# RetNet attention and a SwiGLU block in one kernel: the RMS norm's power taken of three columns with tokens on the partitions, and brought back as rows

## The chip, the cores and the metric

The kernel runs on one core of a Trainium2 chip. The metric is the device time of one execution in microseconds (us), the median of several runs. A core has five engines with queues of their own: TensorE (PE, matrix products; PEld is its weight load), VectorE (DVE), ScalarE (ACT), GpSimd (POOL) and SyncE (SP, which here only issues transfers). Each engine works through its own queue in order; they wait for one another by semaphores. SBUF is the on-chip memory of 128 partitions, PSUM the banks that TensorE writes its products to.

## What is computed

A retention block for 8 batches, 8 heads, 576 tokens and 64 columns a head, then an RMS norm and a SwiGLU block over the 4608 tokens that come of it (512 columns, 1536 inner columns). The reference, cut to what matters:

```python
scores = scale * np.matmul(q, k.transpose(0, 1, 3, 2))        # per batch and head
Dmat = np.where(rel >= 0, gamma[:, None, None] ** rel, 0.0)   # causal decay
x = np.matmul(scores * Dmat, v)                               # -> (4608 tokens, 512)

rms = np.sqrt(np.mean(x * x, axis=-1, keepdims=True) + 1e-06)
xn = x / rms * rms_g
g = xn @ w_gate
silu = g * (1.0 / (1.0 + np.exp(-g)))
out = silu * (xn @ w_val) @ w_out
```

The change touches only the lines with `rms` and `xn`: one power (mean of squares + 1e-6) to -0.5 for each of the 4608 tokens, and the multiplication of x by it.

## The kernel before

**Tiles.** All values are fp32. The tokens are worked through in 12 units (u = 0 to 11) of U = 384 tokens. Within a unit x lies transposed: model columns on the 128 partitions, in four tiles c of 128 columns each, tokens along the row (`x[:, c]` is 128x384). A sum over a token's 512 columns is therefore a sum over partitions.

**Attention** is cut into 32 jobs (batch, pair of heads), worked in `slot(j)`: scores and states of job j, values and carried part of job j-1, then the transposes of job j+1 (`prepare`) and the loads of job j+2 (`load`). The last step of a job writes its columns of x for the units that its tokens belong to.

**The SwiGLU block of a unit.** `up(u, m, g)` runs six times (i = 0 to 5: three groups g, gate and value). Each is seven block products of a Strassen-like scheme, named x, y, z, x, w, z, w after their PSUM banks, each of four matrix products of 128x192; the trace shows eight instructions for one block product, since an fp32 product is two instructions. Sums and differences of the products are DVE's, SiLU is ACT's. Then `down(u, s)` runs three times (s = 0, 1, 2), each 12 products of 128x512 (24 instructions) into one bank, a copy by ACT and a transfer out.

**The norm of the next unit** is spread over the end of a unit by `behind(u, i)`: `norm_0(u+1)` is written after the sixth `up`, `norm_1(u+1)` after `down(u, 0)`, `norm_2(u+1)` after `down(u, 1)`; `down(u, 2)` comes after that, and then `up(u+1)`. For u = 0 the three follow one another with nothing between.

- `norm_0` squares the four tiles on ACT and adds them on DVE (three additions) to one tile of 128x384.
- `norm_1` multiplies that by a matrix of 1/512 on TensorE (L298), so that each partition of the bank `ms` holds the means of all 384 tokens; DVE adds 1e-6 (L300, tile `r`), and POOL raises the 128x384 elements to -0.5 (L301).
- `norm_2` multiplies x by the gain and by `r` (L307, four DVE instructions), and forms the four differences that the block products need (L316, tile `sums` and x in place).

**What sets the order.** The program is written out in the order of its instructions: each engine gets its own in the order in which the loops above write them, and nothing reorders them. `SLOTS` says after which i of a unit a slot of the attention stands: units with u % 3 = 0 have four (after i = 0, 2, 4, 5), u % 3 = 1 has one (after i = 6, which is `down(u, 0)`, and ahead of `norm_1`), u % 3 = 2 has three (1, 3, 5).

**Weights.** The weights come in 36 chunks and are decoded on DVE and ACT from 64-bit words (`exponent`, `mantissa`, `join`), with some sums on POOL (L502). This ends within unit 0 and is written between the pieces of its `up`.

**PSUM.** Five banks of one pool are taken in turn by `bank(...)`; three more hold the scores.

Of the kernel before, what the change touches and what calls it, by code (L numbers as in the profile page):

```python
# [8 lines left out]

F32 = mybir.dt.float32  # L10
U32 = mybir.dt.uint32
AF = mybir.ActivationFunctionType
ALU = mybir.AluOpType
P = 128
# [6 lines left out]
def _decay_tables(H, D):  # L21

    pairs = _gamma(H).reshape(H // 2, 2).T
    rows = np.repeat(pairs, D, axis=0)
    pos = np.arange(P)
    twice = np.concatenate([pos, pos])
    t = rows[:, :, None] ** twice / np.sqrt(D), pairs.T[None] ** -pos[:, None, None], rows ** -(pos % D)[:, None], rows**P
    return [np.ascontiguousarray(x).astype(np.float32) for x in t]  # L30


def _causal_tables():

    t = np.triu(np.ones((P, P), np.float32))
    return [t, np.ascontiguousarray(np.tile(t[: P // 2, : P // 2], (2, 1)))]
# [3 lines left out]
def kernel(  # L40
# [11 lines left out]
    nc = tc.nc  # L52
    B, H, S, D = q.shape
    NTOK, DM = out.shape
# [7 lines left out]
    SQ = 32  # L62
    U = 384
    HU = U // 2
    NU = NTOK // U
    NH = NF // 2
    NG = NH // 2
    EPS = 1e-6
    assert (D, DM, NHP * P) == (64, H * D, DM) and S % SQ == 0 and NTOK % U == 0
    assert NC == NFULL + 1 and TAIL == 64 and AC * P == U and NHP == 4 and NH % 2 == 0  # L70
    assert (2 * S) % U == 0 and B % 2 == 0 and S == 3 * HU

    const = ctx.enter_context(tc.tile_pool(name="const", bufs=1))
# [4 lines left out]
    tmp = ctx.enter_context(tc.tile_pool(name="tmp", bufs=6))  # L78
# [4 lines left out]
    def bank(name):  # L83
        return banks.tile([P, 512], F32, tag="b", name=name)

    def temp(name):
        return tmp.tile([P, U], F32, tag="t", name=name)

    def cell(name, value):
        t = const.tile([P, 1], F32, name=name)  # L90
        nc.vector.memset(t, value)
        return t

    ones = const.tile([P, P], F32, name="ones")
    mhalf = cell("mhalf", -0.5)
    least = cell("least", -896.0)
    most = cell("most", 255.0)
# [8 lines left out]
    rms_g = const.tile([P, NHP], F32, name="rms_g")  # L106
    w_out = const.tile([P, NF, DM], F32, name="w_out")
    o_all = const.tile([P, 2, DM], F32, name="o_all")
# [15 lines left out]
    x_of, t_of, h_of = {}, {}, {}  # L124
# [3 lines left out]
    def load(j):  # L128
        b, hp = jobs[j]
        for nm, src in (("q", q), ("k", k)):  # L130

            t = raw.tile([P, S // SQ, SQ], F32, tag=nm + "raw", name=f"{nm}raw_{j}")
            for e in range(2):
                rows = src[b, 2 * hp + e].rearrange("(t b) (i a) -> i b t a", b=SQ, a=SQ)
                for i in range(D // SQ):
                    r = e * D + i * SQ
                    nc.sync.dma_start(out=t[r : r + SQ], in_=rows[i])
            st[j][nm + "raw"] = t


        for nm, src, bufs in (("k", k, 2), ("v", v, 3)):
            t = raw.tile([P, NFULL, 2, D], F32, tag=nm, name=f"{nm}_{j}", bufs=bufs)
            for e in range(2):
                nc.sync.dma_start(
                    out=t[:, :, e],
                    in_=src[b, 2 * hp + e, : NFULL * P].rearrange("(c p) d -> p c d", p=P),
                )
            st[j][nm] = t
        t = st[j]["vt"] = raw.tile([P, D], F32, tag="vt", name=f"vt_{j}", bufs=3)
        for e in range(2):  # L150
            nc.sync.dma_start(
                out=t[e * TAIL : e * TAIL + TAIL], in_=v[b, 2 * hp + e, NFULL * P :]
            )

    def prepare(j):

        d = st[j]
        hp = jobs[j][1]
        for nm in ("q", "k"):
            t = att.tile([P, S], F32, tag=nm + "T", name=f"{nm}T_{j}")  # L160
            nc.vector.transpose(out=t, in_=d.pop(nm + "raw").rearrange("p t a -> p (t a)"))  # L161
            d[nm + "T"] = t
        for e in range(2):
            t = d["v"][:, :, e]
            nc.scalar.activation(out=t, in_=t, func=AF.Copy, scale=gv[:, hp, e : e + 1])
        nc.scalar.activation(out=d["vt"], in_=d["vt"], func=AF.Copy, scale=gt[:, hp : hp + 1])
# [76 lines left out]
    def carried(j):  # L243
# [4 lines left out]
        for c in range(1, NC):  # L248
# [4 lines left out]
            )  # L253
        for q0 in range(0, S, HU):
            blk, o = divmod(q0, AC * P)
            u, c0 = divmod(b * S + q0, U)
            if u not in x_of:
                x_of[u] = xp.tile([P, NHP, U], F32, tag="x", name=f"x_{u}")
            nc.vector.tensor_tensor(
                out=x_of[u][:, hp, c0 : c0 + HU], in0=av[blk][:, o : o + HU],  # L260
                in1=gq[:, hp, q0 % P : q0 % P + HU], op=ALU.mult,
            )
        st[j] = {}

    def slot(j):

        if j > len(jobs):
            return
        if j < len(jobs):
            scores(j)  # L270
            states(j)
        if j > 0:
            values(j - 1)
        if j < len(jobs):
            weigh(j)
        if j > 0:
            carried(j - 1)
        if j + 1 < len(jobs):
            prepare(j + 1)
        if j + 2 < len(jobs):  # L280
            load(j + 2)
# [13 lines left out]
    def norm_1(u):  # L295

        ms = bank(f"ms_{u}")
        nc.tensor.matmul(ms[:, :U], lhsT=ones, rhs=t_of[u], start=True, stop=True)  # L298
        r = t_of[u] = temp(f"r_{u}")
        nc.vector.tensor_scalar(out=r, in0=ms[:, :U], scalar1=EPS, scalar2=None, op0=ALU.add)  # L300
        nc.gpsimd.tensor_tensor(out=r, in0=r, in1=mhalf.to_broadcast([P, U]), op=ALU.pow)  # L301

    def norm_2(u):

        x = x_of[u]
        for c in range(NHP):
            nc.vector.scalar_tensor_tensor(  # L307
                out=x[:, c], in0=x[:, c], scalar=rms_g[:, c : c + 1], in1=t_of[u],
                op0=ALU.mult, op1=ALU.mult,
            )  # L310
        b11, b12 = x[:, :2, :HU], x[:, :2, HU:]
        b21, b22 = x[:, 2:, :HU], x[:, 2:, HU:]
        t = ffn.tile([P, 3, 2, HU], F32, tag="sums", name=f"sums_{u}")
        t2, t3, t4 = (t[:, i] for i in range(3))
        for o, a, b in ((t3, b22, b12), (b12, b12, b11), (t2, b22, b12), (t4, b21, t2)):
            nc.vector.tensor_tensor(out=o, in0=a, in1=b, op=ALU.subtract)  # L316

        t_of[u] = b11, b21, b12, t4, t2, t3, b22
# [62 lines left out]
    def down(u, s):  # L381
        ps = bank(f"out_{u}_{s}")
        for f in range(NF):
            nc.tensor.matmul(  # L384
                ps[:, :DM], lhsT=h_of[u][:, f, s * P : s * P + P], rhs=w_out[:, f],
                start=(f == 0), stop=(f == NF - 1),
            )
        o = o_all[:, (u * (U // P) + s) % 2]
        nc.scalar.copy(out=o, in_=ps[:, :DM])  # L389
        nc.sync.dma_start(out=out[u * U + s * P : u * U + s * P + P, :], in_=o)  # L390

# [48 lines left out]
    def load_chunks(n):  # L440

        nonlocal n_loads
        while n_loads < min(n, len(chunks)) and waits_at.get(spare(n_loads)) is None:
            load_chunk(n_loads)
            n_loads += 1
# [74 lines left out]
    with tc.manual_schedule():  # L520
        load(0)
        tables = zip((gq, gv, gt, gc, causal, causal_t), (*_decay_tables(H, D), *_causal_tables()))
        for t, values_ in tables:
            name = t.tensor.name + "_table"
            nc.scalar.dma_start(out=t, in_=nc.inline_tensor(values_, name=name).ap())
        nc.scalar.dma_start(out=rms_g, in_=moe_rms_g.rearrange("(c p) -> p c", p=P))
        for t in sd:
            nc.gpsimd.memset(t, 0.0)
        nc.vector.memset(ones, 1.0 / DM)
        load_chunks(WAHEAD)  # L530
        prepare(0)
        load(1)
        exponent(0)
        exponent(1)
        mantissa(0)
        for j in range(NHP + 1):
            slot(j)
            weights_to(2 * j)
        for part in (norm_0, norm_1, norm_2):
            part(0)  # L540
        step = 0

        def behind(u, i):
            at, n = SLOTS[u % 3]
            if i in at:
                slot(u // 3 * 8 + n + at.index(i))
            if u + 1 < NU and 5 <= i < 8:
                (norm_0, norm_1, norm_2)[i - 5](u + 1)

        for u in range(NU):  # L550
            for i in range(2 * NG):
                g, m = divmod(i, 2)
                weights_to(4 * i + 4)
                for _ in up(u, m, g):
                    step += 1
                    weights_to(8 + 2 * step // 3)
                behind(u, i)
            weights_to(len(chunks))
            for s in range(U // P):
                down(u, s)  # L560
                behind(u, 2 * NG + s)

# [26 lines left out]
```

## Time and profile before

| what | value |
|---|---|
| median of 3 runs | 1875.89 us (1874.83 to 1876.75) |
| the profiled execution: own time, span | 1874.94 us, 1872.9 us |
| PE busy | 1228.9 us, 66% of the span |
| POOL busy | 772.5 us, 41%, in 42 instructions |
| DVE busy, ACT busy | 605.4 us (32%), 298.2 us (16%) |
| mean granted TensorE clock | 0.832 of full speed |

The span runs from the first to the last instruction of the profiled execution; 2.0 us of its own time lie outside. Busy shares are means over stages that differ, so they are read together with the waits: which engine stood still, for whom, how long and how often. A row of the waits names the waiting engine and line, then the one that released it, then the total, the number of times and the longest. A row of the groups has line, engine, operation, output and inputs with their shapes and the count; behind the bar the busy time in us, the mean of one in ns, and the idle time of that engine just ahead of them with its releaser. A row of the timeline has start and duration in us, engine, line, operation, and in brackets the idle time ahead of it.

### The profile page before, as it was taken

Reading aid. Unit: us, or ns where it says so; the run is one execution under the profiler, and the core shown is the slowest. Engines: PE = TensorE matmul, PEld = TensorE weight load, DVE = VectorE, ACT = ScalarE, POOL = GpSimd, SP = SyncE. Lnnn points to the kernel's source line nnn. Section 1 sums busy time; section 2 is a strip of 40 time slices with the busy share of each in tenths; the row PEclk is TensorE's granted clock in tenths of the full one; section 3 lists DMA queues with packets and bytes.
Section 4 is the critical chain, followed back from the end, with each engine's and each line's share of the span. In section 5 each row is a group of like instructions: output and inputs, shape, how many; then the busy total and the mean of one; then the engine's idle time right before and its main releaser. Section 6 shows DMA issues by size and latency. Waiting matters only on the chain.

```text
span 1872.9 us, 17016 instructions
## 1 busy us (share of the span) xinstructions
PE 1228.9 (66%) x6968; PEld 979.0 (52%) x6968; DVE 605.4 (32%) x1185; ACT 298.2 (16%) x570; POOL 772.5 (41%) x42
## 2 busy tenths in 40 slices
PE   3207657396397399198199099199099189379199
PEld 3206553393393295194195096096097087176095
DVE  5507881141251153142152053042054054032041
ACT  3404451010021021011021022011012021011010
POOL 0492306607506604805704802902902901923900
PEclk9657878698699699599599599699599699789599
DMA  8604441001021023001022022001012010000000
GB/s 172 137 0 115 125 115 41 0 1 42 0 50 42 0 50 66 1 1 42 0 38 49 6 50 61 6 1 36 6 26 55 11 26 6 11 1 12 6 1 17
DMA packets 245310, 66.77 MB, mean 36 GB/s; under 512 B 226544, under 2 KB 238960, under 8 KB 245232
## 3 DMA queue, kind: packets, MB, share of 16 engines
q1 hardware_dynamic: 229440, 46.17, 12.0%
q10 hardware_dynamic: 15792, 19.51, 3.4%
q8 instruction: 55, 0.90, 0.2%
q14 instruction: 23, 0.19, 0.0%
HBM read 56.21 MB, written 9.44 MB: 35 GB/s over the span
## 4 chain that ended last, share of the span: by engine, by line
PE 46%; POOL 36%; DVE 9%; POOLq 3%; ACT 3%; DMA 1%; issue 1%; SPq 0%; DVEq 0%; ACTq 0%
POOL r L301 36%; PE w L336 9%; PE z L336 9%; PE x L336 9%; PE out L384 8%; PE y L336 5%; POOLq L584 3%; PE s L186 2%; PE av L236 2%; DVE x L307 1%; PE av L250 1%; DVE exp L481 1%; ACT exp L458 1%; ACT exp L457 1%; ACT exp L461 1%
## 5 line engine op out<-in xcount | busy, mean ns | idle before, releaser
L301 POOL TENSOR_TENSOR r<-r,mhalf 128x384 f32<-128x384 f32 x12 | 738.2, 61519 | 873.5 <-DVE r L300 873.5
L336 PE MATMUL x<-x,w_gate 128*128 128x192 f32 x576 | 127.1, 371 | 551.4 <-DVE x L307 537.6
L336 PEld LDWEIGHTS x<-x,w_gate 128*128 128x128 f32 x576 | 111.0, 219 | 563.0 <-issue 547.5
L384 PE MATMUL out<-w_out,h 128*128 128x512 f32 x864 | 374.9, 593 | 0.0
L384 PEld LDWEIGHTS out<-w_out,h 128*128 128x128 f32 x864 | 163.5, 190 | 198.6 <-issue 195.6
L307 DVE SCALAR_TENSOR_TENSOR x<-x,rms_g,r 128x384 f32<-128x384 f32 x48 | 26.5, 614 | 740.4 <-POOL r L301 740.4
L360 ACT COPY m<-x 128x384 f32<-128x384 f32 x72 | 34.0, 472 | 701.5 <-PE x L336 701.5
L336 PE MATMUL w<-sums,w_val 128*128 128x192 f32 x576 | 110.9, 338 | 12.1 <-DVE c L343 12.1
L336 PE MATMUL x<-x,w_val 128*128 128x192 f32 x576 | 109.5, 334 | 8.6 <-ACT m L360 8.6
L336 PE MATMUL w<-sums,w_gate 128*128 128x192 f32 x576 | 108.9, 333 | 8.2 <-DVE h L343 8.2
L336 PE MATMUL z<-x,w_val 128*128 128x192 f32 x576 | 105.9, 327 | 2.3 <-DVE u L343 2.3
L336 PEld LDWEIGHTS w<-sums,w_val 128*128 128x128 f32 x576 | 100.4, 198 | 13.2 <-DVE c L343 13.2
L336 PE MATMUL z<-x,w_gate 128*128 128x192 f32 x576 | 105.5, 326 | 0.3 <-DVE u L343 0.3
L336 PEld LDWEIGHTS w<-sums,w_gate 128*128 128x128 f32 x576 | 98.3, 195 | 9.1 <-DVE h L343 9.1
L336 PEld LDWEIGHTS x<-x,w_val 128*128 128x128 f32 x576 | 96.1, 193 | 10.8 <-ACT m L360 10.8
L336 PEld LDWEIGHTS z<-x,w_val 128*128 128x128 f32 x576 | 95.9, 191 | 2.7 <-issue 2.7
L336 PEld LDWEIGHTS z<-x,w_gate 128*128 128x128 f32 x576 | 95.6, 190 | 1.0 <-issue 1.0
L186 PE MATMUL s<-qT,kT 64*128 64x128 f32 (+1 forms) x640 | 52.2, 304 | 34.8 <-DVE kT L161 34.8
L389 ACT COPY o_all<-out 128x512 f32<-128x512 f32 x36 | 21.1, 585 | 331.6 <-PE out L384 331.6
L343 DVE TENSOR_TENSOR u<-m,y 128x384 f32<-128x384 f32 x72 | 39.9, 554 | 103.3 <-PE y L336 95.3
L355 ACT ACTIVATE h<-h 128x384 f32<-128x384 f32 x108 | 56.1, 521 | 97.5 <-DVE h L343 97.5
L343 DVE TENSOR_TENSOR h<-u,w 128x384 f32<-128x384 f32 x72 | 39.9, 554 | 90.1 <-PE w L336 90.1
(70 smaller groups left out, 1217.5 us busy)
## 6 DMA issues: line engine op xcount, KB each, us to landing
qraw<-in_q_dram SPq DMA_DIRECT2D x128, 72.0 KB, 2.4
kraw<-in_k_dram SPq DMA_DIRECT2D x128, 72.0 KB, 2.5
out_dram<-o_all SPq DMA_DIRECT2D x36, 256.0 KB, 2.0
k<-in_k_dram SPq DMA_DIRECT2D x64, 128.0 KB, 2.8
v<-in_v_dram SPq DMA_DIRECT2D x64, 128.0 KB, 2.8
w_out<-in_moe_w_gate_dram ACTq DMA_DIRECT2D x12, 512.0 KB, 4.7
w_out<-in_moe_w_val_dram ACTq DMA_DIRECT2D x12, 512.0 KB, 3.5
w_out<-in_moe_w_out_dram ACTq DMA_DIRECT2D x9, 512.0 KB, 3.5
```

The lines of the kernel that those rows point to most:

```text
L186: nc.tensor.matmul(s[:, e, ck] if c < NFULL else s[e * n : e * n + n, 2, :n], lhsT=d["kT"][r, ck], rhs=d["qT"][r, ck], start=True, stop=True,)
L236: nc.tensor.matmul(av[blk][e * D : e * D + D, o : o + n], lhsT=d["v"][:, c, e] if c < NFULL else d["vt"][r], rhs=d["ret"][:, e, c * P : c ...
L250: nc.tensor.matmul(av[blk][:, o : o + n], lhsT=sd[j % 2][:, c - 1], rhs=d["qT"][:, c * P : c * P + n], start=False, stop=(c in (AC - 1, NC ...
L301: nc.gpsimd.tensor_tensor(out=r, in0=r, in1=mhalf.to_broadcast([P, U]), op=ALU.pow)
L307: nc.vector.scalar_tensor_tensor(out=x[:, c], in0=x[:, c], scalar=rms_g[:, c : c + 1], in1=t_of[u], op0=ALU.mult, op1=ALU.mult,)
L336: nc.tensor.matmul(ps[:, i * HU : i * HU + HU], lhsT=w_up[m][:, 2 * blk + c, cut], rhs=t_of[u][blk][:, c], start=(start and i == c == 0), ...
L343: nc.vector.tensor_tensor(out=o, in0=a, in1=pairs_of(ps), op=ALU.add)
L355: nc.scalar.activation(out=o, in_=c, func=AF.Silu)
L360: nc.scalar.copy(out=s1, in_=pairs_of(x_))
L384: nc.tensor.matmul(ps[:, :DM], lhsT=h_of[u][:, f, s * P : s * P + P], rhs=w_out[:, f], start=(f == 0), stop=(f == NF - 1),)
L389: nc.scalar.copy(out=o, in_=ps[:, :DM])
L584: with tile.TileContext(nc) as tc:
```

## The change

The power is no longer taken of 128x384 elements, all partitions alike, but of one value a token.

- In `norm_1` the sum over the columns is now made by three products with the squares as the stationary side (128 tokens each) and a single column `mean_w` of 1/512 as the moving side. Their results are three columns of 128 tokens: `ms[:, :3]`, tokens on the partitions. DVE's addition and POOL's power work on 128x3. DVE then makes three diagonal matrices (an identity times the column, as a scalar for each partition) side by side in a 128x384 tile `diag`.
- In `norm_2` TensorE multiplies `diag` by a matrix of ones into another PSUM bank `rb`, which gives back the 384 values on every partition; the four multiplications of x read them from there instead of from SBUF.
- At the start POOL makes the identity (a memset and a select), and DVE one more constant.

```diff
     ones = const.tile([P, P], F32, name="ones")
+    ident = const.tile([P, P], F32, name="ident")
+    mean_w = cell("mean_w", 1.0 / DM)
...
     def norm_1(u):

         ms = bank(f"ms_{u}")
-        nc.tensor.matmul(ms[:, :U], lhsT=ones, rhs=t_of[u], start=True, stop=True)
-        r = t_of[u] = temp(f"r_{u}")
-        nc.vector.tensor_scalar(out=r, in0=ms[:, :U], scalar1=EPS, scalar2=None, op0=ALU.add)
-        nc.gpsimd.tensor_tensor(out=r, in0=r, in1=mhalf.to_broadcast([P, U]), op=ALU.pow)
+        for s in range(NS):
+            nc.tensor.matmul(
+                ms[:, s : s + 1], lhsT=t_of[u][:, s * P : s * P + P], rhs=mean_w,
+                start=True, stop=True,
+            )
+        r = tmp.tile([P, NS], F32, tag="r", name=f"r_{u}", bufs=1)
+        nc.vector.tensor_scalar(out=r, in0=ms[:, :NS], scalar1=EPS, scalar2=None, op0=ALU.add)
+        nc.gpsimd.tensor_tensor(out=r, in0=r, in1=mhalf.to_broadcast([P, NS]), op=ALU.pow)
+        t_of[u] = temp(f"diag_{u}")
+        for s in range(NS):
+            nc.vector.tensor_scalar(
+                out=t_of[u][:, s * P : s * P + P], in0=ident, scalar1=r[:, s : s + 1],
+                scalar2=None, op0=ALU.mult,
+            )

     def norm_2(u):
...
         x = x_of[u]
+        rb = bank(f"rb_{u}")
+        nc.tensor.matmul(rb[:, :U], lhsT=ones, rhs=t_of[u], start=True, stop=True)
         for c in range(NHP):
             nc.vector.scalar_tensor_tensor(
-                out=x[:, c], in0=x[:, c], scalar=rms_g[:, c : c + 1], in1=t_of[u],
+                out=x[:, c], in0=x[:, c], scalar=rms_g[:, c : c + 1], in1=rb[:, :U],
                 op0=ALU.mult, op1=ALU.mult,
             )
...
-        nc.vector.memset(ones, 1.0 / DM)
+        nc.vector.memset(ones, 1.0)
+        make_identity(nc, ident)
```

Here NS = U // P = 3. The change moves instructions in two queues. In TensorE's queue, at the end of unit 2 (names end in the unit and a running number; `out_2_0` is `down(2, 0)`, `x_3` the first products of unit 3), before:

```order
L384 MATMUL out_2_0_2519<-w_out_97,h_2_2003 128x512 x12
L298 MATMUL ms_3_2534<-sq_3_0_2508,ones_79 128x384
L384 MATMUL out_2_1_2539<-w_out_97,h_2_2003 128x512 x12
L384 MATMUL out_2_2_2563<-w_out_97,h_2_2003 128x512 x12
L336 MATMUL x_3_0_0_2579<-x_3_1928,w_gate_99 128x192 x4
L336 MATMUL y_3_0_0_2580<-sums_3_2558,w_gate_99 128x192 x4
```

and with the change:

```order
L401 MATMUL out_2_0_2550<-w_out_100,h_2_2034 128x512 x12
L303 MATMUL ms_3_2565<-mean_w_81,sq_3_0_2539 128x1 x3
L401 MATMUL out_2_1_2576<-w_out_100,h_2_2034 128x512 x12
L322 MATMUL rb_3_2591<-diag_3_2572,ones_79 128x384
L401 MATMUL out_2_2_2602<-w_out_100,h_2_2034 128x512 x12
L353 MATMUL x_3_0_0_2618<-x_3_1951,w_gate_102 128x192 x4
L353 MATMUL y_3_0_0_2619<-sums_3_2597,w_gate_102 128x192 x4
```

A product that depends on POOL's power now stands between `down(2, 1)` and `down(2, 2)`; before, the first such product stood behind both. In DVE's queue at the same place, before:

```order
L292 TENSOR_TENSOR sq_3_0_2508<-sq_3_0_2508,sq_3_2_2512 128x384
L300 TENSOR_SCALAR r_3_2536<-ms_3_2534 128x384
L307 SCALAR_TENSOR_TENSOR x_3_1928<-x_3_1928,rms_g_96,r_3_2536 128x384 x4
L316 TENSOR_TENSOR sums_3_2558<-x_3_1928 128x384
L316 TENSOR_TENSOR x_3_1928<-x_3_1928 128x2x192
```

and with the change:

```order
L296 TENSOR_TENSOR sq_3_0_2539<-sq_3_0_2539,sq_3_2_2543 128x384
L308 TENSOR_SCALAR r_3_2569<-ms_3_2565 128x3
L312 TENSOR_SCALAR diag_3_2572<-ident_80,r_3_2569 128x128 x3
L324 SCALAR_TENSOR_TENSOR x_3_1951<-x_3_1951,rms_g_99,rb_3_2591 128x384 x4
L333 TENSOR_TENSOR sums_3_2597<-x_3_1951 128x384
L333 TENSOR_TENSOR x_3_1951<-x_3_1951 128x2x192
```

Three diagonals stand ahead of the multiplications, and they are what now waits for POOL; the multiplications wait for TensorE. No other work stands between on either side.

More of the change, by code (lines that the diff above doesn't have):

```diff
@@ L8 @@
 from concourse._compat import with_exitstack
+from concourse.masks import make_identity
 F32 = mybir.dt.float32
@@ L64 @@
     HU = U // 2
+    NS = U // P
     NU = NTOK // U
@@ L387, in down @@
             )
-        o = o_all[:, (u * (U // P) + s) % 2]
+        o = o_all[:, (u * (NS) + s) % 2]
         nc.scalar.copy(out=o, in_=ps[:, :DM])
@@ L558 @@
             weights_to(len(chunks))
-            for s in range(U // P):
+            for s in range(NS):
                 down(u, s)
```

## Prediction

> **What bounds the kernel now.** I read the busy shares first, then the waits, then the timeline around one place where TensorE stands still, then that place for every unit. The page's first part:
>
> ```profile
> PE 1228.9 (66%) x6968; PEld 979.0 (52%) x6968; DVE 605.4 (32%) x1185; ACT 298.2 (16%) x570; POOL 772.5 (41%) x42
> ```
>
> TensorE is busy longest, but a third of the span it is not. The view of the waits says for whom, and the groups say what that costs POOL:
>
> ```profile
> DVE x L307 <- POOL r L301: 740.4, 12, 61.7
> PE x L336 <- DVE x L307: 537.6, 12, 63.0
> ...
> L301 POOL TENSOR_TENSOR r<-r,mhalf 128x384 f32<-128x384 f32 x12 | 738.2, 61519 | 873.5 <-DVE r L300 873.5
> ```
>
> TensorE waits 12 times, once a unit, for DVE's multiplication of x, and DVE waits for POOL's power, 61.5 us each time. POOL's own 873.5 us of idle time cost nothing: nobody waits for it to start. The timeline at the end of unit 2 (first TensorE, then POOL, then TensorE again):
>
> ```profile
> 565.94 10.52 PE L384 MATMUL out<-w_out,h 128*128 128x512 f32 x24
> 576.29 0.81 PE L298 MATMUL ms<-sq,ones 128*128 128x384 f32 x2
> 576.94 20.76 PE L384 MATMUL out<-w_out,h 128*128 128x512 f32 x48
> 577.84 61.52 POOL L301 TENSOR_TENSOR r<-r,mhalf 128x384 f32<-128x384 f32 x1 [82.27 <-DVE r L300]
> 640.16 2.90 PE L336 MATMUL x<-x,w_gate 128*128 128x192 f32 x8 [42.46 <-DVE x L307]
> 646.13 1.47 PE L336 MATMUL z<-x,w_gate 128*128 128x192 f32 x8
> ```
>
> Two `down` (20.76 us) cover a third of the power; 42.46 us stay bare. Everywhere else TensorE is the bound: over the stretch behind unit 0 the groups show no wait of it but this one and a half microsecond behind it (474.6 and 5.1 us in all), and a dense stretch has the full clock while the bare one falls to about half (columns: stretch, length, then busy time of PE, PEld, DVE, ACT, POOL, the granted clock, DMA share, GB/s):
>
> ```profile
> L336 PE MATMUL x<-x,w_gate 128*128 128x192 f32 x528 | 113.3, 364 | 474.6 <-DVE x L307 474.6
> L336 PE MATMUL y<-sums,w_gate 128*128 128x192 f32 x264 | 54.8, 355 | 5.1 <-DVE sums L316 5.1
> ...
> 516.00:566.00 50.00, 50.00 (x423) 47.69 (x422) 27.47 (x56) 10.12 (x22) 0.00 (x0) 1.00 0.25 47
> 598.00:640.00 42.00, 0.00 (x0) 0.00 (x0) 0.61 (x2) 0.37 (x1) 41.36 (x1) 0.54 0.02 6
> ```
>
> **The change part by part.**
>
> *The power* goes from 384 to 3 elements a partition. If its time follows the row, it is 61.52 x 3/384 = 0.48 us, and something fixed. The trace has the power at one length only, so its fixed part is not seen; for other POOL work it is small:
>
> ```profile
> L528 POOL MEMSET sd<- 128x512 f32 x2 | 1.0, 524 | 0.3 <-POOLq L573 0.3
> L573 POOL MEMSET const-float32-1.0<- 128x1 f32 x1 | 0.1, 98 | 0.0
> ```
>
> A memset goes from 524 to 98 ns as its row goes from 512 to 1, so about 0.1 us is fixed. I take 0.6 us; the ends are 0.1 us (the memset of one column) and 61.5 us (all of it fixed), and the upper end is the first rival below.
>
> *The chain that takes its place*, in units 1 to 11: three products, DVE's addition, the power, three diagonals, all during `down(u, 1)`; then the product with ones, four multiplications and four differences, during `down(u, 2)`. DVE's pieces have these neighbours, and the last row is the nearest product with few moving columns:
>
> ```profile
> L216 DVE COPY sum<-s 128x64 f32<-128x64 f32 x32 | 6.9, 215 | 0.0
> L529 DVE MEMSET ones<- 128x128 f32 x1 | 0.2, 165 | 0.0
> L453 DVE TENSOR_SCALAR exp<-w_out 128x512 uint32<-128x512 uint32 x33 | 13.7, 419 | 0.0
> L307 DVE SCALAR_TENSOR_TENSOR x<-x,rms_g,r 128x384 f32<-128x384 f32 x48 | 26.5, 614 | 740.4 <-POOL r L301 740.4
> L316 DVE TENSOR_TENSOR sums<-x 128x384 f32<-128x384 f32 x24 | 13.4, 558 | 0.8
> ...
> 519.91 1.10 PE L250 MATMUL av<-qT,sd 128*128 128x128 f32 x8
> 520.85 1.36 PE L336 MATMUL x<-x,w_gate 128*128 128x192 f32 x7
> ```
>
> The addition out of PSUM is at most 0.2 us (the 128x64 copy), a diagonal between 0.17 (memset 128x128) and 0.42 us (four times the row); I take 0.22, nearer to the row of its own size. First half: 0.2 + 0.6 + 3 x 0.22 and some 0.3 us for hand-overs, 1.8 us, under 10.36 us of `down` (half of 20.76, less its tail): 8.6 us to spare. Second half: 0.65 + 4 x 0.61 + 4 x 0.56 = 5.3 us under another 10.36. So the wait goes whole: **474.6 us** over units 1 to 11. Nothing else is late next: DVE has no other work queued behind the diagonals at that place.
>
> *The slow start behind each wait* goes too. With the pipe full, a block product takes 1.30 us; here x and y, from x's start to z's start, take 5.97 us (640.16 to 646.13) instead of 2.60, and part of that is the wait for `sums`, 5.1 us in eleven. Unit 2 (from 496.37) and unit 11, the last:
>
> ```profile
> 496.37 2.90 PE L336 MATMUL x<-x,w_gate 128*128 128x192 f32 x8 [44.94 <-DVE x L307]
> 501.11 1.46 PE L336 MATMUL z<-x,w_gate 128*128 128x192 f32 x8
> 502.41 1.46 PE L336 MATMUL x<-x,w_gate 128*128 128x192 f32 x8
> ...
> 1780.41 2.90 PE L336 MATMUL x<-x,w_gate 128*128 128x192 f32 x8 [42.48 <-DVE x L307]
> 1786.28 1.46 PE L336 MATMUL z<-x,w_gate 128*128 128x192 f32 x8
> ```
>
> Unit 2's wait is 2.5 us longer since the slot behind `down(1, 0)` holds DVE up; 2.5 us fit into the 8.6 to spare. The same subtraction over the eleven units gives 2.14 us (4.74 less 2.60, as from 496.37) to 3.37 us, together **29.3 us**. The idle times are also counted from the modelled end of the last product, 0.16 us behind where the next could start (565.94 + 10.52 against 576.29): **1.8 us** for eleven.
>
> [...]
>
> *TensorE's own added work.* The product `ms` took 0.65 us (576.29 to 576.94). Three products of one moving column are six instructions, each with a load of 128 columns of weights. The nearest row is the carried product, 0.94 us for eight from start to start, 0.118 each: 0.71 us. The lower end is the states' product with half the weights (0.51 us for 16 in the same slot), 0.19 us; the upper end is six bare weight loads of 0.19 us, 1.14 us. Rows for both:
>
> ```profile
> 518.16 0.69 PE L196 MATMUL s<-v,k 128*64 128x64 f32 x16
> 518.67 1.04 PE L236 MATMUL av<-ret,v 128*64 128x128 f32 x16
> ...
> L336 PEld LDWEIGHTS z<-x,w_gate 128*128 128x128 f32 x576 | 95.6, 190 | 1.0 <-issue 1.0
> ```
>
> The product with ones has the shape of the old `ms`, 0.65 us. Added a unit: 0.71 + 0.65 - 0.65 = 0.71 us, times eleven **7.8 us** (2.1 to 12.5).
>
> *Unit 0* has no `down` ahead of it, so its chain is bare before and after:
>
> ```profile
> 80.20 1.65 PE L298 MATMUL ms<-sq,ones 128*128 128x384 f32 x2 [17.19 <-DVE sq L292]
> 82.52 61.53 POOL L301 TENSOR_TENSOR r<-r,mhalf 128x384 f32<-128x384 f32 x1 [3.39 <-DVE r L300]
> 144.09 2.21 DVE L307 SCALAR_TENSOR_TENSOR x<-x,rms_g,r 128x384 f32<-128x384 f32 x4 [61.64 <-POOL r L301]
> 144.85 2.90 PE L336 MATMUL x<-x,w_gate 128*128 128x192 f32 x8 [63.01 <-DVE x L307]
> ```
>
> From `ms`'s end at 81.85: addition 0.2, power 0.6, diagonals 0.66, the product with ones at the cold 1.65, the first multiplications 0.76, hand-overs 0.3; x starts at about 86.0 instead of 144.85: **58.9 us**. What follows in unit 0 is not bound by TensorE but by the decoding of weights on DVE, which stands in the same queue behind the norm, so it moves forward as it is:
>
> ```profile
> 82.50:144.85 62.35, 0.00 (x0) 0.03 (x1) 0.77 (x2) 0.00 (x0) 61.53 (x1) 0.50 0.00 0
> 144.85:295.00 150.15, 104.37 (x618) 89.99 (x619) 124.75 (x231) 75.41 (x122) 22.56 (x16) 0.83 0.45 118
> ```
>
> No transfer ran during the first wait (DMA share 0.00), so nothing was loaded under its cover that would now be late.
>
> *The identity* is a memset and a select on POOL in the first microseconds. POOL's next work comes much later, and up to that long the edit is free:
>
> ```profile
> 50.86 5.42 POOL L502 TENSOR_TENSOR w_gate<-w_gate 128x512 f32<-128x512 f32 x4 [49.15 <-DVE w_gate L489]
> ```
>
> *The sum*, against the profiled execution's own 1874.94 us: 474.6 + 29.3 + 1.8 - 7.8 + 58.9 = 556.8, which leaves 1318.1. The median lay 0.95 us above that execution; I say **1319 us**.
>
> **The rivals.**
>
> 1. *The power does not shrink with its row* (a price for the instruction, or a large fixed part). Then the change does not do what it says, and more: TensorE's product with ones stands ahead of `down(u, 2)`, so only one `down` covers the power instead of two. With all 61.5 us fixed, TensorE would stand still for 0.2 + 61.5 + 0.66 + 0.3 less 10.36, 52.3 us, instead of 43.1 a unit, and have 0.71 us more work: 11 x 9.9 = 109 us, and in unit 0 some 2.6 us: about **1987 us**, slower. It decides from a fixed part of about 9 us, where the cover ends; each microsecond more costs 11 to 12 us, and at about 52 us the gain is gone. Against it: the memsets, and four subtractions of 512 columns in 5.42 us on the same engine. For it: no row shows a short power. 3 in 100, most of that at prices of some tens of us, so half of it slower.
>
> 2. *The clock falls when TensorE no longer rests.* The trace has no dense stretch over about 100 us, and the change makes one of over a millisecond. Against it: 1.00 was granted in the dense rows, and the fall to half follows idle time, not work. Units 1 to 11 would last about 1061 us (1318.1 less 86.0, 150.15 and two `down` of unit 0); at 0.9 they would take 118 us more: **1437 us**. [...] 5 in 100.
>
> 3. *The waits come back elsewhere*: with 46 us less between units, loads of q, k and v or a DVE hand-over come late at the first slot of a unit. Against it: the two closest slots in the trace are 13.4 us apart and TensorE waits for neither, and between slots of different units at least two `down` (20.76 us) remain:
>
> ```profile
> 704.72 2.10 SPq L137 DMA_DIRECT2D qraw<-in_q_dram  x4
> 718.16 1.96 SPq L137 DMA_DIRECT2D qraw<-in_q_dram  x4
> ```
>
> At 5 us a unit, **1374 us**. 4 in 100.
>
> 4. *Unit 0 keeps part of its wait* because three chunks of weights that lay ready would come one after another; unit 0 decodes 28 of the 36 chunks in 150.15 us, 5.4 us each, so three late ones make **1334 us**. 6 in 100.
>
> **How the numbers follow.** 82 in 100 for the forecast. The bounds of the small costs move it by 6 us down and 5 up, unit 0 by perhaps 8; with rival 4 and the near side of rival 3 the range is 1306 to 1350. Two runs of this kernel can be told apart at about 0.2%; all cases but half of rival 1 are far faster: 0.975 faster, 0.005 within 0.2%, 0.02 slower.
>
> **What would show it.** POOL's power under 1 us and TensorE's wait for the multiplications gone from the list of waits except once, some 4 us, in unit 0; `rb` without idle time ahead of it; the first x and y of each unit at 1.30 us from start to start; dense rows at a clock of 1.00. It would be wrong if `rb` shows idle time (rival 1), if dense rows show less than 1.00 (rival 2), or if any wait of several us recurs eleven times (rival 3).

## The result, and the profile after

The changed kernel takes **1324.34 us** (median of 4 runs, 1322.71 to 1325.02) against 1876.32 us (median of 4 runs beside it, 1874.83 to 1880.03): 0.7055 of the time, 95% interval 0.7042 to 0.7067. A second series (run 7 below) gave 1323.71 us and 0.7048 (0.7038 to 0.7057). The forecast was 1319 us, and 1306 to 1350 as its range.

The profiled execution took 1325.02 us, with a span of 1323.2. Busy times on the page of the changed kernel:

```profile
PE 1214.7 (92%) x7040; PEld 973.0 (74%) x7040; DVE 608.6 (46%) x1222; ACT 298.1 (23%) x570; POOL 44.8 (3%) x44
```

TensorE does as much as before (1214.7 against 1228.9 us), in 550 us less. Next the waits of the changed kernel: the only ones that TensorE has in the norm behind its first product, each with a count of one, in unit 0; then the group of POOL's power and the row of DVE's diagonals (shortest, median and longest in ns, first and last start):

```profile
PE rb L322 <- DVE diag L312: 2.0, 1, 2.0
PE x L353 <- DVE x L324: 0.7, 1, 0.7
PE y L353 <- DVE sums L333: 0.5, 1, 0.5
...
L309 POOL TENSOR_TENSOR r<-r,mhalf 128x3 f32<-128x3 f32 x12 | 10.2, 852 | 1027.3 <-DVE r L308 1027.3
...
L312 DVE TENSOR_SCALAR diag<-ident,r x36: 279/282/288, 87.9 to 1214.0; 128x128 f32<-128x128 f32 x36
```

A power takes 0.85 us instead of 61.5, and the 537.6 and 5.6 us that TensorE waited for the multiplications and the differences have become 3.2, the wait for the diagonals among them. (The norm's first product still waits once for the sum of the squares, 18.5 us ahead of unit 0, as it did before with 17.2.) The end of unit 0 on TensorE's timeline shows the place where it stood still for 42 us before:

```profile
242.59 0.72 PE L303 MATMUL ms<-mean_w,sq 128*128 128x1 f32 x6
243.18 10.55 PE L401 MATMUL out<-w_out,h 128*128 128x512 f32 x24
253.56 0.81 PE L322 MATMUL rb<-diag,ones 128*128 128x384 f32 x2
254.21 10.46 PE L401 MATMUL out<-w_out,h 128*128 128x512 f32 x24
264.51 1.46 PE L353 MATMUL x<-x,w_gate 128*128 128x192 f32 x8
265.81 1.46 PE L353 MATMUL y<-sums,w_gate 128*128 128x192 f32 x8
```

No bracket, so no idle time: `ms`, `down`, the product with ones, `down` and the first products of unit 1 follow one another, and x and y begin 1.30 us apart, here and in the ten units behind. DVE's rows at the same place, the second with its wait for POOL, show how much cover is left:

```profile
243.35 0.16 DVE L308 TENSOR_SCALAR r<-ms 128x3 f32<-128x3 f32 x1 [4.71 <-PE ms L303]
244.50 0.68 DVE L312 TENSOR_SCALAR diag<-ident,r 128x128 f32<-128x128 f32 x3 [0.98 <-POOL r L309]
254.41 2.19 DVE L324 SCALAR_TENSOR_TENSOR x<-x,rms_g,rb 128x384 f32<-128x384 f32 x4 [9.23 <-PE rb L322]
```

The diagonals end at 245.18 (244.50 + 0.68), 8.4 us ahead of the product that reads them at 253.56. And a stretch of 1030 us (PE, PEld, DVE, ACT, POOL, granted clock, DMA share, GB/s), dense from end to end, at the full clock:

```profile
270.00:1300.00 1030.00, 1030.00 (x5992) 830.63 (x5991) 425.85 (x864) 182.61 (x380) 8.49 (x10) 1.00 0.15 32
```

### The profile page after: what moved, and what is told of

The parts are those of the page before. It is cut to its first block, busy times and chain, and to the rows that moved or that the text cites. A ratio compares the mean times of both kernels' runs of the same rounds, so it can differ in the third digit from the quotient of the medians.

```text
span 1323.2 us, 17197 instructions
## 1 busy us (share of the span) xinstructions
PE 1214.7 (92%) x7040; PEld 973.0 (74%) x7040; DVE 608.6 (46%) x1222; ACT 298.1 (23%) x570; POOL 44.8 (3%) x44
## 4 chain that ended last, share of the span: by engine, by line
PE 83%; DVE 7%; DMA 4%; ACT 4%; SPq 1%; issue 1%; ACTq 0%; POOL 0%; DVEq 0%
PE out L401 28%; PE w L353 13%; PE x L353 13%; PE z L353 13%; PE y L353 7%; PE s L190 3%; PE av L240 2%; PE av L254 2%; DMA kraw<-in_k_dram 2%; DVE exp L498 1%; PE s L200 1%; ACT exp L475 1%; ACT exp L474 1%; ACT exp L478 1%; SPq L141 1%; DMA w_out<-in_moe_w_gate_dram 1%
## 5 line engine op out<-in xcount | busy, mean ns | idle before, releaser
L353 PE MATMUL x<-x,w_gate 128*128 128x192 f32 x576 | 111.0, 338 | 14.8 <-ACT m L377 14.1
L353 PEld LDWEIGHTS x<-x,w_gate 128*128 128x128 f32 x576 | 99.0, 197 | 22.9 <-ACT m L377 15.7
L353 PEld LDWEIGHTS z<-x,w_val 128*128 128x128 f32 x576 | 95.8, 191 | 2.7 <-issue 2.6
L190 PEld LDWEIGHTS s<-qT,kT 64*128 64x128 f32 (+1 forms) x640 | 43.8, 203 | 51.3 <-issue 31.9
L228 ACT ACTIVATE sd<-sum,gc 64x256 f32<-64x256 f32 x64 | 32.4, 506 | 204.4 <-DVE sum L222 203.7
L212 DVE TENSOR_TENSOR ret<-s,causal 128x1024 f32<-128x1024 f32 x32 | 39.1, 1223 | 77.3 <-PE av L240 77.3
```

Source lines behind the costliest of these rows:

```text
L190: nc.tensor.matmul(s[:, e, ck] if c < NFULL else s[e * n : e * n + n, 2, :n], lhsT=d["kT"][r, ck], rhs=d["qT"][r, ck], start=True, stop=True,)
L212: nc.vector.tensor_tensor(out=ret.rearrange("p e (c k) -> p e c k", c=NFULL), in0=s[:, :2].rearrange("p e (c k) -> p e c k", c=NFULL), in1 ...
L228: nc.scalar.activation(out=sd[j % 2][r, :, r], in_=t[r], func=AF.Copy, scale=gc[r, hp : hp + 1])
L353: nc.tensor.matmul(ps[:, i * HU : i * HU + HU], lhsT=w_up[m][:, 2 * blk + c, cut], rhs=t_of[u][blk][:, c], start=(start and i == c == 0), ...
```

## The experiments

Three questions were put: is the cover of one `down` what makes the power free (runs 1 to 4), what does bringing the values back cost (runs 5, 7 and 8), and where do the five microseconds come from by which unit 0 starts later than it was forecast to (runs 6, 7 and 9 to 12).

**1. The power of 48 columns.** The three columns are repeated 16 times ahead of the power; the first three are used.

```diff
-        r = tmp.tile([P, NS], F32, tag="r", name=f"r_{u}", bufs=1)
-        nc.vector.tensor_scalar(out=r, in0=ms[:, :NS], scalar1=EPS, scalar2=None, op0=ALU.add)
-        nc.gpsimd.tensor_tensor(out=r, in0=r, in1=mhalf.to_broadcast([P, NS]), op=ALU.pow)
+        r = tmp.tile([P, NPOW], F32, tag="r", name=f"r_{u}", bufs=1)
+        nc.vector.tensor_scalar(
+            out=r.rearrange("p (a s) -> p a s", s=NS),
+            in0=ms[:, :NS].unsqueeze(1).to_broadcast([P, NPOW // NS, NS]),
+            scalar1=EPS, scalar2=None, op0=ALU.add,
+        )
+        nc.gpsimd.tensor_tensor(out=r, in0=r, in1=mhalf.to_broadcast([P, NPOW]), op=ALU.pow)
```

> The changed kernel with the power taken of 48 columns a partition instead of 3 (the three columns repeated 16 times, the first three used). The changed kernel's trace has the power of three columns at 0.85 us, the one before that of 384 at 61.52 us; a straight line through both gives 0.37 us and 0.159 us a column, 8.0 us for 48, so 7.2 us more. Theory (the power lies under one `down`, and TensorE's product with ones waits for nothing until that cover is used up): in the changed kernel's trace the last diagonal ends 8.3 us ahead of that product in eight units and 5.8 us ahead in the three units with a slot behind the first `down`; so 7.2 us are paid in unit 0 and 1.4 us in three units, 11 to 12 us in all: about 1337 us. Rival (the chain is not covered, each microsecond of the power is paid twelve times): 86 us more, about 1411 us.

Measured: 1335.67 us (one execution), 11.3 us above the changed kernel's 1324.34. The power's group and TensorE's wait for the diagonals in this run:

```profile
L314 POOL TENSOR_TENSOR r<-r,mhalf 128x48 f32<-128x48 f32 x12 | 96.1, 8008 | 960.7 <-DVE r L309 960.7
PE rb L327 <- DVE diag L317: 13.4, 4, 9.2
```

8.0 us as the straight line of the forecast has it, and four waits: unit 0 with 9.2 us, and the three units behind a slot with 4.2 us together (1.4 us each). Twelve powers became 86 us longer, and the kernel 11 us, as forecast.

**2. The power of 96 columns.** The same edit with 96.

> The same with 96 columns: 15.7 us by the line, 14.8 us more. Theory: 14.8 us in unit 0, 6.5 us bare in eight units and 9.0 us in three, 94 us in all, and up to 2 us a unit where the clock falls during the wait: 1419 to 1441 us. If the clock does not fall in gaps of 6 to 9 us, the low end; if it does, the x and the `down` behind the gap are slow for some microseconds.

Measured: 1444.51 us, 3.5 us above the range. The waits, and TensorE at the end of unit 0:

```profile
PE rb L327 <- DVE diag L317: 96.1, 12, 16.9
...
258.63 10.55 PE L406 MATMUL out<-w_out,h 128*128 128x512 f32 x24
275.64 1.62 PE L327 MATMUL rb<-diag,ones 128*128 128x384 f32 x2 [6.46 <-DVE diag L317]
277.05 11.36 PE L406 MATMUL out<-w_out,h 128*128 128x512 f32 x24
288.25 1.46 PE L358 MATMUL x<-x,w_gate 128*128 128x192 f32 x8
```

Now every unit waits: 6.46 us here, 6.5 in seven more and 9.1 in the three behind a slot, as forecast. And the clock falls: 0.933 was granted on the mean of this execution, 0.962 in run 1 and 0.961 in the changed kernel. Where it falls, the kernel before shows: 0.54 was granted in the gap of 42 us ahead of unit 3, 0.51 over the 6.0 us from the start of that unit's x on (640.2 to 646.2 us) and 1.00 over the next 5.8 us. Here the product with ones takes 1.41 us from start to start instead of 0.65, the `down` behind it 11.20 instead of 10.30, 1.66 us together. Ahead of unit 11 the same subtraction gives 1.51 us (starts at 1245.33, 1246.74 and 1257.79). Over all eleven units it is 23.0 us, 2.1 on the mean: from unit 1's x to the end this run takes 1154.5 us and the changed kernel 1058.7, 95.8 less; the ten waits there are 72.8 us and their modelled ends 1.6, which leaves 21.4, and the first unit adds 1.66.

The miss of 3.5 us is in part this price, 23.0 us where the range had at most 22. Another 1.8 us is that the idle times are counted from a modelled end, 0.16 us behind where the next product could start, in eleven units. The last 0.7 us stays open.

**3. 96 columns, with the product with ones and the multiplications of x one `down` later.**

```diff
+    NORM = (5, 6, 8)
...
-            if u + 1 < NU and 5 <= i < 8:
-                (norm_0, norm_1, norm_2)[i - 5](u + 1)
+            if u + 1 < NU and i in NORM:
+                (norm_0, norm_1, norm_2)[NORM.index(i)](u + 1)
```

> The same 96 columns, but the product with ones and the multiplications of x written behind the third `down` instead of the second. Theory (the place of that product decides how much cover the power has): two `down` cover it, 8.3 + 10.4 = 18.7 us against 14.8 us, so no unit waits for the power; instead the multiplications and differences stand bare ahead of x and y, about 2.8 us a unit (4.1 us from the first multiplication to the last difference less one block product of 1.3 us): 1325 + 14.8 + 31 = 1371 us. Rival (the place does not matter, the power's length does): as the run with 96 columns, 1419 us or more.

Measured: 1370.92 us, 74 us less than with the same power in run 2. What stands bare now are the multiplications and differences:

```profile
275.77 0.81 PE L328 MATMUL rb<-diag,ones 128*128 128x384 f32 x2
277.29 1.77 PE L359 MATMUL x<-x,w_gate 128*128 128x192 f32 x8 [0.71 <-DVE x L330]
280.73 1.54 PE L359 MATMUL y<-sums,w_gate 128*128 128x192 f32 x8 [1.68 <-DVE sums L339]
```

Only unit 0 still waits for the diagonals (16.9 us); no later unit does. So the place of one product decides whether 15.6 us of power are covered. The price of the later place is what stands bare, some 32 us (46.6 us above the changed kernel, of which the longer power of unit 0 makes 14.8). With a power of 0.85 us there is nothing to gain for it; that the later place would then be the worse one is worked out from these rows and was not run.

**4. The power of 384 columns.** As run 1, with 384 (the tile comes from the pool of 128x384 tiles).

> The changed kernel with the power of 384 columns, as long as before the change: the first rival of the prediction made true (columns, diagonals and the product with ones stay). Theory: power 61.5 us, 60.7 us more than now; 52.3 us bare in eight units and 54.9 in three, 583 us, 61 us in unit 0, 15 to 30 us of slow start: 1985 to 2000 us, so slower than before the change by about 6%, since one `down` less covers the power. Rival (gain and loss come from the length of the power alone, wherever it is waited for): the time before, 1876 us, plus some 10 us of added products.

Measured: 2000.08 us, against 1879.8 us of the kernel before beside it: 6.4% slower with a power of the same 61.52 us. This is the first rival of the prediction made true, 13 us above the price that it was given (1987 us).

```profile
L314 POOL TENSOR_TENSOR r<-r,mhalf 128x384 f32<-128x384 f32 x12 | 738.2, 61519 | 980.2 <-DVE r L309 980.2
PE rb L327 <- DVE diag L317: 650.5, 12, 63.1
```

TensorE waits 650.5 us for the diagonals where it waited 537.6 us for x: of the two `down` that covered the power one now stands behind the wait.

**5. The short power alone.** The kernel before, with the power on three of its 384 columns.

```diff
-        nc.gpsimd.tensor_tensor(out=r, in0=r, in1=mhalf.to_broadcast([P, U]), op=ALU.pow)
+        nc.gpsimd.tensor_tensor(
+            out=r[:, :3], in0=r[:, :3], in1=mhalf.to_broadcast([P, 3]), op=ALU.pow
+        )
```

> The kernel before with one edit: the power is taken of the first 3 of the 384 columns only, the others stay without it (the norm is left out for 381 of 384 tokens). No columns, no diagonals, no product with ones: the shortened power alone, without the price of bringing the values back. Theory (the gain is the power's wait, and the bringing back costs only TensorE's added products): in the changed kernel's trace the three products take 0.59 us and the product with ones 0.65 us, against 0.65 us for the old product, so 0.59 us a unit less here, 6.5 us, and some 2 to 3 us less in unit 0: 1314 to 1319 us against 1324. Rival (the diagonals and the multiplications out of PSUM hold the units up too): 20 us or more below the changed kernel.

Measured: 1310.29 us, 14 us below the changed kernel (13.4 below run 7, beside it), lower than the range. Stage by stage against the changed kernel's profile: behind the start of unit 1's x 1051.8 us instead of 1058.7 (6.9 us, where the added products make 6.5 by their rows); in unit 0 from the norm's product to x 3.99 us instead of 5.77; and 3.9 us because that product itself starts at 81.39 instead of 85.29; the other 2.3 us lie in unit 0 behind its x. From unit 1 on, the bringing back costs about what its products cost. The earlier start is the subject of runs 6 and 9 to 12.

**6. The identity and the constant alone, not used**, in the kernel before.

```diff
+    ident = const.tile([P, P], F32, name="ident")
+    mean_w = cell("mean_w", 1.0 / DM)
     mhalf = cell("mhalf", -0.5)
...
+        make_identity(nc, ident)
         load_chunks(WAHEAD)
```

> The kernel before with the identity and the extra constant made at the start and not used. In the changed kernel's trace unit 0's first product of the norm starts at 85.3 us, in that of the kernel before at 80.2 us. Theory A (the identity on POOL or the constant holds up the start): that product starts at 85 us here too, and the time is about 1881 us. Theory B (the loads at the start land at times that vary from execution to execution): it starts at any time between 79 and 86 us, and the runs of the changed kernel with other lengths of the power differ among themselves by as much.

Measured: 1881.2 us against 1878.49 (1875.53 to 1879.83 in 9 runs), and unit 0's product at 84.2 us. Theory A's numbers came, but theory B allows 84.2 us as well, so this run alone decides nothing.

**7. The changed kernel again.**

> The changed kernel again, for the comparison with the next one and for a second look at unit 0's start: 1322 to 1326 us; the first product of the norm between 79 and 86 us by theory B of the run before, at 85 us by theory A.

Measured: 1323.71 us (1322.26 to 1324.97), the product at 83.6 us: between the start before (80.2) and theory A's 85, so this run does not decide either.

**8. No power at all: seven DVE instructions on rows**, in the kernel before.

```diff
-        nc.vector.tensor_scalar(out=r, in0=ms[:, :U], scalar1=EPS, scalar2=None, op0=ALU.add)
-        nc.gpsimd.tensor_tensor(out=r, in0=r, in1=mhalf.to_broadcast([P, U]), op=ALU.pow)
+        a, t = temp(f"a_{u}"), temp(f"nt_{u}")
+        nc.vector.tensor_scalar(out=a, in0=ms[:, :U], scalar1=EPS, scalar2=None, op0=ALU.add)
+        nc.vector.tensor_scalar(
+            out=r.bitcast(U32), in0=a.bitcast(U32), scalar1=-0.5, scalar2=1597463007.0,
+            op0=ALU.mult, op1=ALU.add,
+        )
+        for _ in range(2):
+            nc.vector.tensor_tensor(out=t, in0=r, in1=r, op=ALU.mult)
+            nc.vector.scalar_tensor_tensor(
+                out=t, in0=t, scalar=-0.5, in1=a, op0=ALU.mult, op1=ALU.mult
+            )
+            nc.vector.scalar_tensor_tensor(
+                out=r, in0=t, scalar=1.5, in1=r, op0=ALU.add, op1=ALU.mult
+            )
```

(The edit makes eight instructions, the addition among them.)

> The kernel before with the power replaced by seven DVE instructions on rows of 384: a first guess from the bits of the mean, and two Newton steps. The whole norm is computed; no POOL, no columns, no diagonals, no product with ones. Theory: the DVE chain is about 0.56 + 0.4 + 6 x 0.6 = 4.6 us, under two `down` (20.8 us); TensorE has 0.59 us a unit less than in the changed kernel, 6.5 us, and unit 0 about 1 us more: about 1319 us, 0.4% below the changed kernel. Rival (TensorE's added products are hidden in some other wait, or DVE's longer chain meets the slots): the same as the changed kernel or above it.

Measured: 1314.87 us (1313.79 to 1316.00 in 5 runs), 0.6999 of the time before (0.6990 to 0.7009), where the changed kernel beside it has 0.7048 (0.7038 to 0.7057): 8.8 us faster, and the intervals do not meet. That is also 4 us below the forecast. The chain in unit 0, and TensorE at the end of unit 0:

```profile
83.58 0.56 DVE L301 TENSOR_SCALAR a<-ms 128x384 f32<-128x384 f32 x1 [1.74 <-PE ms L298]
84.18 0.36 DVE L302 TENSOR_SCALAR r<-a 128x384 uint32<-128x384 uint32 x1
88.13 2.21 DVE L319 SCALAR_TENSOR_TENSOR x<-x,rms_g,r 128x384 f32<-128x384 f32 x4
...
240.37 0.81 PE L298 MATMUL ms<-sq,ones 128*128 128x384 f32 x2
241.02 20.76 PE L396 MATMUL out<-w_out,h 128*128 128x512 f32 x48
261.62 1.46 PE L348 MATMUL x<-x,w_gate 128*128 128x192 f32 x8
```

The chain is 4.55 us of DVE (83.58 to 88.13). It is bare in unit 0, where it makes the way from the norm's product to x 1.2 us longer (7.00 us against 5.77); from unit 1 on it lies under two `down`. Behind unit 1's start this kernel takes 1052.6 us against 1058.6 in run 7: 6.0 us, where 6.5 us of products were forecast. The other 2.8 us of the medians do not show in these two traces: the profiled executions are the slowest of this series and the fastest of run 7's, 6.2 us apart, and x of unit 1 starts at 261.62 and 261.76 us.

**9 to 12. Four edits of that kernel for the start.** Run 9 adds the identity as in run 6, without the constant; run 10 has the same but writes the identity just ahead of unit 0's norm; run 11 adds the constant alone; run 12 adds two memsets onto a tile that is there.

Run 9 adds to run 8's kernel:

```diff
+    ident = const.tile([P, P], F32, name="ident")
     mhalf = cell("mhalf", -0.5)
...
+        make_identity(nc, ident)
         load_chunks(WAHEAD)
```

Run 10 has the tile too, and the call elsewhere:

```diff
+        make_identity(nc, ident)
         for part in (norm_0, norm_1, norm_2):
             part(0)
```

Run 11 has only the constant, run 12 only the memsets:

```diff
+    mean_w = cell("mean_w", 1.0 / DM)
     mhalf = cell("mhalf", -0.5)
```

```diff
             nc.gpsimd.memset(t, 0.0)
+            nc.gpsimd.memset(t[:, 0], 0.0)
```

> The Newton kernel with the identity made at the start and not used. In seven traces with the identity, unit 0's first product of the norm starts at 83.2 to 85.3 us, in three without it at 80.2 to 81.9. Theory A (the identity costs the start some 3 us): it starts at 83 to 85 us, and the median is 1317 to 1319 us against 1314.9 without it. Theory B (the ten traces fell so by chance): 80 to 82 us or anything between, and the median 1314 to 1316.

> The same with the identity written just ahead of unit 0's norm: the tile has its place in SBUF as before, but POOL does not work on it while the first loads run. Theory A1 (POOL's two instructions at the start disturb the first loads): product at 80 to 82 us, median 1314 to 1316. Theory A2 (it is the tile's 512 bytes a partition, which move the tiles that are loaded behind it): 83 to 85 us, 1317 to 1319.

> The Newton kernel with only the extra constant of one column made on DVE at the start (4 bytes a partition and one memset of 0.06 us). Theory A1 and B: 80 to 82 us, 1314 to 1316. Theory A2: the tiles move by a little here as well, so if any move is enough, 83 to 85 us and 1317 to 1319.

> The Newton kernel with two more POOL memsets of 128x128 at the start, onto a tile that is there already; nothing moves in SBUF. Theory A1: 83 to 85 us, 1317 to 1319. Theory A2 and B: 80 to 82 us, 1314 to 1316.

Measured, beside run 8 (the product's start from one trace each):

| run | edit | unit 0's product starts | median of runs |
|---|---|---|---|
| 8 | none | 81.9 us | 1314.87 us |
| 9 | identity | 80.9 us | 1314.39 us |
| 10 | identity, late | 81.6 us | 1313.18 us |
| 11 | constant | 83.8 us | 1316.42 us |
| 12 | two memsets | 81.0 us | 1314.17 us |

Theory A falls for the identity, and with it A1 (POOL's work at the start) and, for the identity's 512 bytes, A2 (its place). The one edit that delays the start is the constant of one column, whose own work is one DVE memset of 0.06 us. It costs 1.9 us against run 8's trace and 1.6 us of the medians. What is known of it stands in the last section.

## Why the prediction was right, step by step

- **The bound** (TensorE waits for DVE's multiplication, that for POOL): right. With the power short, 540 us of TensorE's waits are gone, and no other wait of TensorE came up in their place.
- **The power** was put at 0.6 us and takes 0.85. Through 3, 48, 96 and 384 columns (0.852, 8.008, 15.618 and 61.519 us) it is 0.37 us and 0.159 us a column; the fixed part was taken from memsets as 0.1 us, about a quarter of what the power has. It cost 0.25 us, once, in unit 0.
- **The chain under one `down`, 8.6 us to spare**: 8.3 to 8.4 us in eight units and 5.8 in the three behind a slot, and runs 1 and 2 show that this is where the cover ends.
- **The slow start behind each wait**, 29.3 us, is gone: x and y at 1.30 us in each unit from 1 on. This size was taken from the rows of the kernel before. Less the wait for `sums` it is 2.2 us a wait, and run 2 (2.1) and run 4 (2.3) measured about the same on another product. Units 1 to 11 were forecast at 1058.5 us of the span (1316.1 less 86.0, 139.2 and 32.4 for unit 0; the prediction's 1061 holds 2.0 us outside the span and 0.7 of unit 0 as well) and last 1058.7 (264.51 to 1323.2). That they agree to 0.2 us is in part luck: the added products cost some 1.3 us less than forecast, and the gains came out smaller by about as much.
- **TensorE's added work**, 0.71 us a unit: the three products take 0.59 us and the product with ones 0.65 where one product of 0.65 stood, so 0.59 us were added. Runs 5 and 8, which leave it out, gain 6.9 and 6.0 us behind unit 1's start; forecast were 7.8.
- **Unit 0's chain**: 5.77 us from its first product to x (85.29 to 91.06); forecast were 5.8 (80.20 to 86.0). Here too small errors cancel: the power is 0.25 us longer, the first products 0.21 us shorter (1.44 against 1.65).

```profile
85.29 1.44 PE L303 MATMUL ms<-mean_w,sq 128*128 128x1 f32 x6 [18.49 <-DVE sq L296]
91.06 2.93 PE L353 MATMUL x<-x,w_gate 128*128 128x192 f32 x8 [0.71 <-DVE x L324]
```

- **The step that was off**: that everything up to unit 0's norm stays as it is. The norm's first product starts 5.1 us later than before in the profiled execution (85.29 against 80.20), and unit 0 takes 2.0 us longer from x to its first `down` (141.2 against 139.2). These 7.1 us are the whole difference between the forecast span of 1316.1 and 1323.2. Of the 5.1 us, some 2 to 4 come from the constant (1.9 between the traces of runs 11 and 8, 4.0 between run 6 and the kernel before, 3.1 between the means of the eight traces with it and the six without); the rest, and the 2.0 us, lie within what traces differ by among themselves (83.2 to 85.3 us with the constant; 139.6 to 141.1 us in runs 5, 7 and 8), and their cause stays open. The prediction priced the identity at nothing and does not name the constant at all. Its range held 8 us for unit 0, so the median stayed well inside.
- **The rivals**: the first is settled by run 4 (its price was 13 us too low, its condition isn't met); the clock was 1.00 over 1030 us; no wait came back; unit 0 behind its x is 2.0 us longer and not 16. (Of the four instructions that the first rival calls subtractions one is an addition; their time is as read.)

## What to carry to other kernels

When one instruction on one engine holds up all others, ask first how its time depends on the shape, and give it the values in the shape that it is fast in. Here the columns and the diagonals cost 1.24 us of TensorE a unit, 0.59 more than the one product before, against 61.5 us of power. Then ask what its consumer now stands ahead of: the same edit with a long power would have been 6% slower, because it moves the wait ahead of a `down` that had covered it. And where an engine that has time to spare does the same work with a few instructions on rows (4.6 us of DVE here), no detour is needed at all: that version is 0.7% faster than the changed kernel. A square root and a division, as the reference has them, were not run.

## What was not expected of the hardware

**A constant of one column made the loads some 3% slower.** In the built programs every constant of one column takes 32 bytes a partition. In six of the traced kernels the targets of the loads begin at multiples of 64 bytes (`w_out` at 26240, `qraw` at 140928 in the kernel before); in the eight traces with `mean_w` they begin 32 bytes off (26784 and 141472 in the changed kernel). The identity takes 512 bytes and shifts nothing in that sense. The packets' time on the queue of the q, k and v loads, which also holds the transfers out (its share times the span, a mean over the 16 DMA engines), and the start of unit 0's norm fall into two groups without an exception:

| kernels | targets | time of the packets of queue q1 | unit 0's product starts |
|---|---|---|---|
| before; runs 5, 8, 9, 10, 12 | at 64 bytes | 224.7 to 226.0 us | 80.2 to 81.9 us |
| changed kernel (twice); runs 1, 2, 3, 4, 6, 11 | 32 bytes off | 231.8 to 233.7 us | 83.2 to 85.3 us |

The queue's rows on the pages of run 10 and of run 11 (packets, MB, share), whose spans are 1311.4 and 1314.1 us:

```profile
q1 hardware_dynamic: 229440, 46.17, 17.2%
```

```profile
q1 hardware_dynamic: 229440, 46.17, 17.7%
```

The same packets take about 3% longer, and the start, where the DMA share is 0.85 to 0.91 over the first 77 us, becomes some 2 to 4 us longer. That it is a boundary in memory, and not something else about this constant, is argued from the addresses; a kernel with 32 bytes of padding more was not run. Nor is it shown which boundary: in the first group the targets quoted are multiples of 128 bytes as well, and q and k arrive in pieces of 32 values, 128 bytes.

**What the clock's fall cost varied from unit to unit, and hardly with a wait of 6.5 to 55.3 us.** Behind 6.5 to 9.1 us it cost 2.1 us on the mean of eleven units (run 2), and 1.51 and 1.66 us in two of them. Behind 52.7 to 55.3 us it cost 2.3 us on the mean of eleven (run 4). In the kernel before, behind 42.4 to 45.0 us, it was 2.14 to 3.37 us with some 0.5 us of the wait for `sums` in it. The two means differ by 0.2 us and the units of the kernel before by 1.2, so no growth with the wait is shown; what makes one unit dearer than another is not shown either. Behind run 1's three waits of 1.4 us the cost was 0.07 us each (its 1063.6 us from unit 1's x to the end less 1058.7, 4.2 of waits and 0.5 of modelled ends). The first of run 4's eleven, 2.33 us:

```profile
366.67 1.62 PE L327 MATMUL rb<-diag,ones 128*128 128x384 f32 x2 [52.66 <-DVE diag L317]
368.08 12.03 PE L406 MATMUL out<-w_out,h 128*128 128x512 f32 x24
```

(From start to start, 1.41 us less 0.65; and 11.87 less 10.30, x of the next unit starting at 379.95.)
